# Cross-covariance attention into a channel mix: q and k kept apart in their tile, v loaded ahead, and the rows of batch 1 taken earlier

## The chip, the cores and the metric

The kernel runs on one core of a Trainium2 chip. The metric is device time of one execution in microseconds (us). Before the change three runs took 515.36, 516.77 and 517.39 us; the median is 516.77 us.

## The reference

Two layers follow one another. B is 4, N 6208, C 256; the hidden width of the second layer is 1024.

```python
qn = q / (norm(q, axis=1) + 1e-6)           # over the 6208 rows
kn = k / (norm(k, axis=1) + 1e-6)
s  = kn.transpose(0, 2, 1) @ qn / tau       # 256 x 256 for each batch
a  = softmax(s)                             # over the last axis
x  = v @ a                                  # B x N x C
xk = mu_k * x + (1 - mu_k) * x_prev         # x_prev: x one row earlier, 0 at row 0
xr = mu_r * x + (1 - mu_r) * x_prev
out = sigmoid(xr @ w_r) * (relu(xk @ w_k) ** 2 @ w_v)
```

For each batch all rows of q and k must have been read before its 256 x 256 matrix `a` exists, and `a` is needed for the first row of x.

## The kernel before, in words

The 6208 rows of a batch are 12 blocks of 512 rows and 64 rows that are left. q and k are read in *groups*: group 0 holds the 64 left rows, the others 512 rows (the last two groups of batch 0 hold 256 each). In a group, partition p holds four consecutive rows, so a group is four *units* (rows in the words of the change) of 128 rows of q and k; a unit is two matmuls into `s_ps` (L167) and, for every second unit, one squaring by ScalarE (`unit_square`, L150), which is added to the running sum of squares `acc` by VectorE (`next_add`, L154).

Batch 0 comes first and alone: its q and k are read as fp32 by SyncE's queue and cast by VectorE (`group_cast`, L131). For batches 1 to 3 GpSimd's queue reads q and k and casts to bf16 on the way (L125). It also loads v (`v_load`, L311), again with a cast. A loaded block of v is transposed: blocks 0 to 2 by TensorE (`v_transpose_pe`), later ones by a DMA transpose from SyncE's queue (`v_transpose`, L318).

The main loop has one *pass* for each i from -2 on, with eight *steps* j from 0 to 7; step (i, j) is named so below. In pass i the kernel computes `up` for block i+1 (x_k times w_k, eight pieces, L419, with a relu by ScalarE, L423, and a squaring by VectorE, L429), `down` for block i (x_r times w_r, L444, and the squared hidden layer times w_v, L448), the output of block i (tanh on ScalarE, L457; product on VectorE, L458), and x and the mixes for block i+2 (`x_half`, L348; `mix`, L404). Between these it takes units of the next batch: the tuple `slots` says in which steps, and `unit()` calls `loads_upto()`, which loads q/k groups up to three ahead of the unit. Every engine works its instructions in the order in which they are written here; the program waits only through semaphores.

The first five units of batch 1 (`early`) have their matmuls in pass -1 and their squares in passes 0 and 1 (L641). When the last unit of a batch is done, sixteen pieces (`softmax_pieces`: `evac` copies `s_ps` out, L254; `fold`, `norms`, `roots`, `roots2`, `invert`, `spread`, `scale`, `exp`, `weigh`) are done one a step. They end in `a_sb`, which `x_half` needs for the first block of the next batch, two passes after the pieces start.

Buffers that matter: five `qk` tiles, five `v_bf`, four `vT`, one `s_ps` for batches 1 to 3 (so the next batch's first matmul has to follow `evac`). GpSimd's DMAs use eight semaphores in turn, so that each of its DMAs is issued after the one eight places earlier has landed. In its queue before the loop stand: v of block 0, w_k, group 0 of batch 1 (q, then k), v of block 1, group 1, w_r, w_v, v of block 2, group 2 (L564 to L571).

Of the kernel before, what the change touches and what calls it, by code (L numbers as in the profile page):

```python
# [10 lines left out]
F32 = mybir.dt.float32  # L11
BF16 = mybir.dt.bfloat16
AX = mybir.AxisListType.X
AF = mybir.ActivationFunctionType
OP = mybir.AluOpType
# [3 lines left out]
def kernel(  # L19
# [13 lines left out]
    nc = tc.nc  # L33
    B, N, C = q.shape
    D = C
    DF = moe_w_k.shape[1]
    P = 128
    M = 512
    S = M // P
    assert C == 256 and DF == 1024  # L40
    NB = N // M
    L = N - NB * M
# [44 lines left out]
    sums = {}  # L87
# [15 lines left out]
    def qk_src(t, b, g):  # L103
        if g == 0:
            return t[b, NB * M:, :].rearrange("(p j) c -> p j c", j=1)
        r = P * sum(sizes(b)[1:g])
        n = sizes(b)[g]
        return t[b, r:r + P * n, :].rearrange("(p j) c -> p j c", p=P)

    def group_load(b, g):  # L110
        rows, n = rows_of(b, g)
        qk = pq.tile([P, S, 2, C], BF16, name="qk", tag="qk", bufs=5)
        groups[b, g] = (qk,)
        if b == 0:
            qk2 = pq.tile([P, S, 2, C], BF16, name="qk2", tag="qk2", bufs=4)
            groups[b, g] += (qk2,)
            t_f = []
            for i, t in enumerate((q, k)):
                f = pq.tile([P, S, C], F32, name=f"f{i}", tag=f"f{i}", bufs=6)
                nc.sync.dma_start(f[:rows, :n], qk_src(t, b, g))  # L120
                t_f.append(f)
            groups[b, g] += tuple(t_f)
        else:
            for i, t in enumerate((q, k)):
                nc.gpsimd.dma_start(qk[:rows, :n, i, :], qk_src(t, b, g))  # L125

    def group_cast(b, g):
        rows, n = rows_of(b, g)
        qk, qk2, *t_f = groups[b, g]
        for i in range(2):  # L130
            nc.vector.tensor_copy(qk[:rows, :n, i, :], t_f[i][:rows, :n])  # L131
        for i in range(2):
            nc.scalar.activation(qk2[:rows, :n, i, :], t_f[i][:rows, :n], AF.Square)  # L133

    def unit_square(b, g, s):

        rows, n = rows_of(b, g)
        if s % 2:
            return
        qk = groups[b, g][0]  # L140
        if n == 1:
            t = pq.tile([P, 1, 2 * C], BF16, name="sq", tag="sq1", bufs=2)
            sums[b, "left"] = t
        elif (g, s) == (1, 0):
            t = pn.tile([P, 2, 2 * C], F32, name="acc", tag="acc", bufs=2)
            sums[b] = t
        else:
            t = pq.tile([P, 2, 2 * C], F32, name="sq2", tag=f"f{s // 2}", bufs=6)
            adds.append((now[0] + 2, b, t))
        nc.scalar.activation(t[:rows], qk[:rows, s:s + min(n, 2)].rearrange("p s i c -> p s (i c)"), AF.Square)  # L150

    def next_add():
        _, b, t = adds.pop(0)
# [2 lines left out]
    def unit_matmul(b, g, s):  # L156
        rows, n = rows_of(b, g)
        t0 = g == order(b)[0] and s == 0
        te = g == len(sizes(b)) - 1 and s == n - 1
        if t0:  # L160

            cov[b] = (ps.tile([P, 2, C], F32, name="s_ps", tag="s_ps" if b else "vr_ps", bufs=1 if b else 2),
                      ps.tile([P, 2 * C], F32, name="ssq_ps", tag="vr_ps", bufs=2) if b == 0 else None)
        s_ps = cov[b][0] if b or g <= DIRECT else cov["s"]
        qk = groups[b, g][0]
        for ih in range(2):
            nc.tensor.matmul(s_ps[:, ih, :], qk[:rows, s, 1, ih * P:(ih + 1) * P],  # L167
                             qk[:rows, s, 0, :], start=t0 and ih == 0, stop=te,
                             skip_group_check=True)
        if s == n - 1 and b == 0:  # L170
            if g > DIRECT:
                norms_direct(g)
            else:
                group_norms(b, g)
# [23 lines left out]
    def softmax_pieces(b):  # L198
# [18 lines left out]
                                 start=i == 0, stop=False, skip_group_check=True)  # L217

        def fold():
            t = pq.tile([P, 2 * C], BF16, name="sq", tag="sq", bufs=1)  # L220
            nc.vector.tensor_tensor(t, sums[b][:, 0], sums[b][:, 1], op=OP.add)
            sums[b] = t

        def norms():
            bank[b] = ps.tile([P, 2 * C], F32, name="bank", tag="xT_ps", bufs=2)
            for t, rows in ((sums.pop((b, "left"))[:, 0], L), (sums.pop(b), P)):
                for i in range(4):
                    nc.tensor.matmul(bank[b][:, C + i:C + i + 1], t[:rows, i * P:(i + 1) * P], ones[:rows, 0:1],
                                     start=rows == L and i == 0, stop=rows == P, skip_group_check=True)
# [78 lines left out]
    def v_load(i):  # L308
        b, t = blocks[i]
        v_bf = p2.tile([P, S, C], BF16, name="v_bf", tag="v_bf", bufs=5)  # L310
        nc.gpsimd.dma_start(v_bf, v[b, t * M:(t + 1) * M, :].rearrange("(s p) c -> p s c", p=P))  # L311
        st[i, "v"] = v_bf
# [247 lines left out]
    def next_load():  # L560
        group_load(*loads.pop(0))
        pos["ld"] += 1

    nc.gpsimd.dma_start(w_k_sb, moe_w_k.rearrange("(ko ki) f -> ki ko f", ki=P))  # L564
    next_load()
    v_load(1)
    next_load()
    nc.gpsimd.dma_start(w_r_sb, moe_w_r.rearrange("(ko ki) d -> ki ko d", ki=P))
    nc.gpsimd.dma_start(w_v_sb, moe_w_v.rearrange("(fo fi) d -> fi fo d", fi=P))
    v_load(2)  # L570
    next_load()  # L571
    roots()
    evac()
    nc.scalar.activation(gate, ones[:, 0:1], AF.Exp)
# [13 lines left out]
    early = units[:S + 1]  # L588
# [4 lines left out]
    left = {}  # L593
    for i in range(-2, NBLK - 1):
        for j in range(8):
            if j % 2:
                if j == 1 and i >= 1:
                    finish(i - 1, 3)
                elif j > 1 and i >= 0:
                    finish(i, j // 2 - 1)  # L600
            if j == 0 and 3 <= i + 5 < NBLK - 1:
                v_load(i + 5)
            if chain:
                piece = chain[0]
                if len(chain) == FOLD and any(e[1] == holds[0] for e in adds):
                    piece = None
                else:
                    chain.pop(0)
                if piece is not None:
                    piece()  # L610
            if 0 <= i + 1 < NBLK:
                up(i + 1, j)
            if i >= 0:
                if j == 0 :
                    square(i, 7)
            if j > 0 and 0 <= i + 1 < NBLK:
                square(i + 1, j - 1)
            if j > 0 and i >= 0:
                down(i, j - 1)
            elif j == 0 and i >= 1:  # L620
                down(i - 1, 7)
            if i + 2 < NBLK:
                n = i + 2
                full = 0 < n < NBLK - 1
                if j in (0, 2) and full:
                    x_half(n, int(j > 0))
                if j == 3:
                    mix_delta(n)
                if j in (4, 5):
                    mix(n, "xk", int(j > 4))  # L630

            if j in (0, 2) and 0 <= i + 1 < NBLK:
                mix(i + 1, "xr", int(j > 0))
            if i == -1 and j == 6:
                v_transpose_pe(2, nc.vector.tensor_copy)()
            if j == 5 and 3 <= i + 4 < NBLK - 1:
                v_transpose(i + 4)
            if i == -1 and j in (5, 6):
                for u in early[:2] if j == 5 else early[2:]:
                    unit_matmul(*u)  # L640
            if (i, j) in ((0, 1), (0, 5), (1, 3)):  # L641
                unit_square(*early[{(0, 1): 0, (0, 5): 1, (1, 3): 3}[i, j]])
            if i < 0:
                slots = ()
            elif i == 0:
                slots = (3, 5, 7)
            elif i == 1:
                slots = (1, 2, 4, 5, 7)
            elif i < 8:
                slots = (1, 2, 3, 4, 5, 7)  # L650
            else:
                slots = (3, 5, 7) if (i - 8) % NB == 0 else (1, 3, 4, 5, 7) if (i - 8) % NB < 3 else (1, 3, 5, 7)
            if j in slots and pos["mm"] < len(units):
                unit()
            if adds and adds[0][0] <= now[0] and (j in (1, 6, 7) or adds[0][1] == holds[0] and chain):
                next_add()
            now[0] += 1
            if i >= 0 and i % NB == 2 and j == 1 and i // NB < B:
                left_go[0] = left_x(i // NB)
            if i >= 0 and i % NB == 4 and j == 4 and i // NB < B:  # L660
                left_go[0][0]()
            if i >= 0 and i % NB == 6 and j == 4 and i // NB < B:
                left_go[0][1]()
# [36 lines left out]
```

## Time and profile before

| what | value |
|---|---|
| median of three runs | 516.77 us (515.36 to 517.39) |
| the profiled execution | 517.02 us, of which its span is 515.2 |
| PE busy | 490.6 us, 95% |
| DVE (VectorE) busy | 457.2 us, 89% |
| ACT (ScalarE) busy | 431.3 us, 84% |
| POOL (GpSimd) busy | 104.6 us, 20% |
| POOL's DMA queue (q0) | 65808 packets, 33.01 MB |
| SyncE's DMA queue (q1) | 77712 packets, 49.98 MB |

PE is TensorE, PEld its weight loads. Busy time of PE overstates how near it is to its peak, because matmuls are pipelined. Bytes of a casting load are counted as they are written, in bf16; twice as many are read.

### The profile page before, as it was taken

The page shows a single profiled execution, that of the slowest core. Times are in us where ns is not written, and L with a number is a line of the kernel's source. Part 1 is how long each engine was busy: PE and PEld are TensorE (multiplying, and loading weights), DVE is VectorE, ACT ScalarE, POOL GpSimd, SP SyncE. Part 2 cuts the span into 40 slices and gives each one's busy share as a digit, 9 for nine tenths or more (in the row PEclk, how much of TensorE's full clock was granted, in tenths as well). Part 3 has the DMA queues.
Part 4 walks back from the last instruction along what each step waited for, and adds up shares of the span by engine and source line. Part 5 has one row for each costly group of instructions (what it writes and reads, how often), then busy time and mean ns, then how long its engine had stood idle before and what let it go on. Part 6 is the DMA issues. An engine that isn't in the chain of part 4 may idle for free.

```text
span 515.2 us, 9442 instructions
## 1 busy us (share of the span) xinstructions
PE 490.6 (95%) x3447; PEld 333.2 (65%) x3509; DVE 457.2 (89%) x788; ACT 431.3 (84%) x858; POOL 104.6 (20%) x143
## 2 busy tenths in 40 slices
PE   3988899999999999999999999999999999999996
PEld 1453666666666667667666667677666666666665
DVE  3557899999999999999999999999989788888884
ACT  5887889988988889888988898898878887878884
POOL 0045242213242321311243231210030101000000
PEclk9989999999999999999999999999999999999999
DMA  8999999999989999879899999965269676424123
GB/s 298 420 316 181 192 160 192 208 196 193 154 122 188 208 163 190 144 125 193 130 150 188 189 164 169 182 115 130 62 108 178 109 142 117 112 70 116 42 83 102
DMA packets 143734, 83.72 MB, mean 162 GB/s; under 512 B 51716, under 2 KB 140104, under 8 KB 143688
## 3 DMA queue, kind: packets, MB, share of 16 engines
q0 software_dynamic: 65808, 33.01, 51.9%
q1 hardware_dynamic: 77712, 49.98, 41.8%
q8 instruction: 27, 0.44, 0.3%
q14 instruction: 19, 0.16, 0.1%
q10 hardware_dynamic: 168, 0.13, 0.1%
HBM read 78.71 MB, written 25.43 MB: 202 GB/s over the span
## 4 chain that ended last, share of the span: by engine, by line
PE 69%; DVE 16%; DMA 9%; ACT 3%; issue 1%; POOL 0%; SPq 0%; DVEq 0%; ACTq 0%; POOLq 0%
PE vr_ps L448 26%; PE kT_ps L419 23%; PE vr_ps L444 8%; PE xT_ps L348 6%; DMA f<-in_k_dram 5%; PE s_ps L167 5%; DVE acc L154 5%; DVE kk L429 4%; DVE xk L404 2%; DMA v_bf<-in_v_dram 2%; DVE res L458 2%; DMA vT<-v_bf 2%; DVE xr L404 1%; DVE delta L394 1%; ACT kr L423 1%
## 5 line engine op out<-in xcount | busy, mean ns | idle before, releaser
L423 ACT ACTIVATE kr<-kT_ps 128x512 bf16<-128x512 f32 (+1 forms) x392 | 233.9, 600 | 41.0 <-PE kT_ps L419 36.9
L448 PE MATMUL vr_ps<-w_v_sb,kk 128*128 128x256 bf16 x1536 | 231.7, 273 | 0.9 <-DVE kk L429 0.3
L419 PE MATMUL kT_ps<-xk,w_k_sb 128*128 128x512 bf16 (+1 forms) x725 | 218.4, 377 | 0.3 <-DVE xk L404 0.2
L448 PEld LDWEIGHTS <-kk 128*128 128x128 bf16 x1536 | 149.5, 98 | 60.1 <-DVE kk L429 3.0
L429 DVE TENSOR_TENSOR kk<-kr 128x1024 bf16<-128x1024 bf16 (+1 forms) x196 | 133.0, 679 | 4.2 <-ACT kr L423 3.3
L458 DVE SCALAR_TENSOR_TENSOR res<-res,vr_ps 128x256 f32<-128x256 f32 x192 | 79.7, 415 | 28.2 <-ACT res L457 27.8
L419 PEld LDWEIGHTS <-w_k_sb 128*128 128x128 bf16 x784 | 76.1, 98 | 28.6 <-issue 0.5
L154 DVE TENSOR_TENSOR acc<-acc,sq 128x1024 f32<-128x1024 f32 x69 | 84.0, 1217 | 0.0
L167 PE MATMUL s_ps<-qk 128*128 128x256 bf16 (+1 forms) x392 | 74.0, 291 | 5.4 <-DVE qk L131 5.4
L457 ACT ACTIVATE res<-vr_ps 128x256 f32<-128x256 f32 x192 | 75.4, 393 | 1.3 <-PE vr_ps L448 1.3
L444 PE MATMUL vr_ps<-w_r_sb,xr 128*128 128x256 bf16 x384 | 73.2, 272 | 3.1 <-DVE res L458 0.4
L350 ACT CAST xT<-xT_ps 128x512 bf16<-128x512 f32 x94 | 55.8, 594 | 23.3 <-PE xT_ps L348 23.1
L150 ACT ACTIVATE sq<-qk 128x1024 f32<-128x1024 bf16 (+1 forms) x72 | 75.2, 1046 | 0.0
L404 DVE SCALAR_TENSOR_TENSOR xr<-delta,mu_t,xT 128x512 bf16<-128x512 bf16 x96 | 71.4, 744 | 0.0
L404 DVE SCALAR_TENSOR_TENSOR xk<-delta,mu_t,xT 128x512 bf16<-128x512 bf16 x96 | 71.3, 745 | 0.0
L444 PEld LDWEIGHTS <-xr 128*128 128x128 bf16 x384 | 37.5, 98 | 45.4 <-issue 1.4
L125 POOL DMA_DIRECT2D qk<-in_q_dram x39 | 28.7, 736 | 181.1 <-ACT kr L423 140.5
L348 PE MATMUL xT_ps<-vT,a_sb 128*128 128x512 bf16 x188 | 56.1, 379 | 4.1 <-DVE a_sb L273 2.2
L311 POOL DMA_DIRECT2D v_bf<-in_v_dram x48 | 37.2, 777 | 67.8 <-DMA vT<-v_bf 62.6
L167 PEld LDWEIGHTS <-qk 128*128 128x128 bf16 (+1 forms) x392 | 39.0, 103 | 17.9 <-DVE qk L131 8.2
L394 DVE TENSOR_TENSOR delta<-xT 128x1024 bf16<-128x1024 bf16 x48 | 32.9, 686 | 0.1
L133 ACT ACTIVATE qk<-f 128x1024 bf16<-128x1024 f32 (+2 forms) x28 | 25.9, 947 | 7.4 <-DMA f<-in_q_dram 4.1
(82 smaller groups left out, 164.1 us busy)
## 6 DMA issues: line engine op xcount, KB each, us to landing
out_dram<-res SPq DMA_DIRECT2D x47, 512.0 KB, 5.2
v_bf<-in_v_dram POOLq DMA_DIRECT2D x48, 256.0 KB, 7.7
qk<-in_q_dram POOLq DMA_DIRECT2D x36, 256.0 KB, 6.3
qk<-in_k_dram POOLq DMA_DIRECT2D x36, 256.0 KB, 7.4
f<-in_q_dram SPq DMA_DIRECT2D x11, 512.0 KB, 8.4
f<-in_k_dram SPq DMA_DIRECT2D x11, 512.0 KB, 9.3
vT<-v_bf SPq DMA_TRANSPOSE x45, 7.9
f<-in_q_dram SPq DMA_DIRECT2D x2, 256.0 KB, 8.3
```

The lines of the kernel that those rows point to most:

```text
L150: nc.scalar.activation(t[:rows], qk[:rows, s:s + min(n, 2)].rearrange("p s i c -> p s (i c)"), AF.Square)
L154: nc.vector.tensor_tensor(sums[b], sums[b], t, op=OP.add)
L167: nc.tensor.matmul(s_ps[:, ih, :], qk[:rows, s, 1, ih * P:(ih + 1) * P], qk[:rows, s, 0, :], start=t0 and ih == 0, stop=te, skip_group_che ...
L348: nc.tensor.matmul(xT_ps, a_sb[:, b, ih, dh * P:(dh + 1) * P], vT[:, :, ih, :], start=ih == 0, stop=ih == 1)
L404: nc.vector.scalar_tensor_tensor(o[:, dh], st[i, "d"][:, dh], mu[:, dh:dh + 1], st[i, "x"][:, dh, :M], op0=OP.mult, op1=OP.add)
L419: nc.tensor.matmul(kT_ps[:, :m], w_k_sb[:, dh, fh * P:(fh + 1) * P], xk[:, dh, :m], start=dh == 0, stop=dh == 1)
L423: nc.scalar.activation(st[i, "kr", fh // 2][:, fh % 2, :m], kT_ps[:, :m], AF.Relu, scale=0.5 ** 0.5)
L429: nc.vector.tensor_tensor(st[i, "kk"][:, fh - 1:fh + 1, :m], kr, kr, op=OP.mult)
L444: nc.tensor.matmul(vr_ps[:, D:], xr[:, dh, s * P:(s + 1) * P], w_r_sb[:, dh, :], start=dh == 0, stop=dh == 1)
L448: nc.tensor.matmul(vr_ps[:, :D], kk[:, fh, s * P:(s + 1) * P], w_v_sb[:, fh, :], start=fh == 0, stop=fh == 7)
L457: nc.scalar.activation(res[:, s], vr_ps[:, D:], AF.Tanh, scale=0.5)
L458: nc.vector.scalar_tensor_tensor(res[:, s], res[:, s], 1.0, vr_ps[:, :D], op0=OP.add, op1=OP.mult)
```

## The change

1. In the tile of a q/k group, q and k stand apart: `[P, 2, S, C]` in place of `[P, S, 2, C]`. A partition's four rows of q are then one run of 2048 bytes in the tile, where there were four of 512, and the same for k. Squares, sums, fold, norms and matmuls are indexed accordingly.
2. GpSimd's queue: v of block 1 stands ahead of group 0, v of block 2 ahead of w_r and w_v, v of block 3 ahead of group 2, and v of block 4 ahead of group 3. Group 2 moves from before the loop to pass -2, group 3 from pass 0 to pass -1.
3. The squares of the early units are taken in steps (0,0), (0,2) and (0,4), not (0,1), (0,5) and (1,3). Pass 0 takes four units, one of them in step 1, where it took three; pass 1 takes six where it took five. All later units come up to two slots earlier, so that the last unit of batch 1 falls in step (7,4) in place of (7,7), that of batch 2 in (19,3) in place of (19,7), that of batch 3 in (31,3) in place of (31,7), and the softmax pieces start accordingly.

```diff
     def group_load(b, g):
-        qk = pq.tile([P, S, 2, C], BF16, name="qk", tag="qk", bufs=5)
+        qk = pq.tile([P, 2, S, C], BF16, name="qk", tag="qk", bufs=5)
...
-                nc.gpsimd.dma_start(qk[:rows, :n, i, :], qk_src(t, b, g))
+                nc.gpsimd.dma_start(qk[:rows, i, :n, :], qk_src(t, b, g))
     def group_cast(b, g):
...
-            nc.vector.tensor_copy(qk[:rows, :n, i, :], t_f[i][:rows, :n])
+            nc.vector.tensor_copy(qk[:rows, i, :n, :], t_f[i][:rows, :n])
     def unit_square(b, g, s):
...
-            t = pq.tile([P, 2, 2 * C], F32, name="sq2", tag=f"f{s // 2}", bufs=6)
+            t = pq.tile([P, 2, 2, C], F32, name="sq2", tag=f"f{s // 2}", bufs=6)
...
-        nc.scalar.activation(t[:rows], qk[:rows, s:s + min(n, 2)].rearrange("p s i c -> p s (i c)"), AF.Square)
+        nc.scalar.activation(t[:rows], qk[:rows, :, s:s + min(n, 2)], AF.Square)
...
         def fold():
-            nc.vector.tensor_tensor(t, sums[b][:, 0], sums[b][:, 1], op=OP.add)
+            nc.vector.tensor_tensor(t, sums[b][:, :, 0], sums[b][:, :, 1], op=OP.add)
...
     nc.gpsimd.dma_start(w_k_sb, moe_w_k.rearrange("(ko ki) f -> ki ko f", ki=P))
-    next_load()
     v_load(1)
     next_load()
+    next_load()
+    v_load(2)
     nc.gpsimd.dma_start(w_r_sb, moe_w_r.rearrange("(ko ki) d -> ki ko d", ki=P))
     nc.gpsimd.dma_start(w_v_sb, moe_w_v.rearrange("(fo fi) d -> fi fo d", fi=P))
-    v_load(2)
-    next_load()
...
             if j == 0 and 3 <= i + 5 < NBLK - 1:
                 v_load(i + 5)
+                if i < 0:
+                    next_load()
...
-            if (i, j) in ((0, 1), (0, 5), (1, 3)):
-                unit_square(*early[{(0, 1): 0, (0, 5): 1, (1, 3): 3}[i, j]])
+            if (i, j) in ((0, 0), (0, 2), (0, 4)):
+                unit_square(*early[{(0, 0): 0, (0, 2): 1, (0, 4): 3}[i, j]])
             if i < 0:
                 slots = ()
             elif i == 0:
-                slots = (3, 5, 7)
-            elif i == 1:
-                slots = (1, 2, 4, 5, 7)
+                slots = (1, 3, 5, 7)
             elif i < 8:
                 slots = (1, 2, 3, 4, 5, 7)
```

More of the change, by code (lines that the diff above doesn't have):

```diff
@@ L141, in unit_square @@
         if n == 1:
-            t = pq.tile([P, 1, 2 * C], BF16, name="sq", tag="sq1", bufs=2)
+            t = pq.tile([P, 2, 1, C], BF16, name="sq", tag="sq1", bufs=2)
             sums[b, "left"] = t
         elif (g, s) == (1, 0):
-            t = pn.tile([P, 2, 2 * C], F32, name="acc", tag="acc", bufs=2)
+            t = pn.tile([P, 2, 2, C], F32, name="acc", tag="acc", bufs=2)
             sums[b] = t
         else:
-            t = pq.tile([P, 2, 2 * C], F32, name="sq2", tag=f"f{s // 2}", bufs=6)
+            t = pq.tile([P, 2, 2, C], F32, name="sq2", tag=f"f{s // 2}", bufs=6)
             adds.append((now[0] + 2, b, t))
-        nc.scalar.activation(t[:rows], qk[:rows, s:s + min(n, 2)].rearrange("p s i c -> p s (i c)"), AF.Square)
+        nc.scalar.activation(t[:rows], qk[:rows, :, s:s + min(n, 2)], AF.Square)
     def next_add():
@@ L166, in unit_matmul @@
         for ih in range(2):
-            nc.tensor.matmul(s_ps[:, ih, :], qk[:rows, s, 1, ih * P:(ih + 1) * P],
-                             qk[:rows, s, 0, :], start=t0 and ih == 0, stop=te,
+            nc.tensor.matmul(s_ps[:, ih, :], qk[:rows, 1, s, ih * P:(ih + 1) * P],
+                             qk[:rows, 0, s, :], start=t0 and ih == 0, stop=te,
                              skip_group_check=True)
@@ L219, in fold @@
         def fold():
-            t = pq.tile([P, 2 * C], BF16, name="sq", tag="sq", bufs=1)
-            nc.vector.tensor_tensor(t, sums[b][:, 0], sums[b][:, 1], op=OP.add)
+            t = pq.tile([P, 2, C], BF16, name="sq", tag="sq", bufs=1)
+            nc.vector.tensor_tensor(t, sums[b][:, :, 0], sums[b][:, :, 1], op=OP.add)
             sums[b] = t
@@ L225, in norms @@
             bank[b] = ps.tile([P, 2 * C], F32, name="bank", tag="xT_ps", bufs=2)
-            for t, rows in ((sums.pop((b, "left"))[:, 0], L), (sums.pop(b), P)):
+            for t, rows in ((sums.pop((b, "left")).rearrange("p i s c -> p (i s c)"), L),
+                            (sums.pop(b).rearrange("p i c -> p (i c)"), P)):
                 for i in range(4):
```

## The prediction

> **What bounds the kernel now.** I read the page first: shares, then the chain that ended last.
>
> ```profile
> PE 490.6 (95%) x3447; PEld 333.2 (65%) x3509; DVE 457.2 (89%) x788; ACT 431.3 (84%) x858; POOL 104.6 (20%) x143
> PE 69%; DVE 16%; DMA 9%; ACT 3%; issue 1%; POOL 0%; SPq 0%; DVEq 0%; ACTq 0%; POOLq 0%
> ```
>
> PE carries most, but DVE (16%) and DMA (9%) carry stages of their own. The busy times by stretch show which:
>
> ```profile
> 50.00:60.00 10.00, 8.74 (x64) 5.78 (x64) 8.32 (x14) 7.56 (x15) 4.46 (x6) 1.00 1.45 196
> 60.00:70.00 10.00, 8.02 (x56) 5.37 (x56) 8.45 (x13) 8.53 (x18) 2.24 (x3) 1.00 1.42 173
> 100.00:120.00 20.00, 19.62 (x139) 13.37 (x140) 20.00 (x33) 17.84 (x36) 5.59 (x8) 1.00 1.40 186
> 200.00:220.00 20.00, 19.89 (x141) 13.81 (x142) 19.58 (x34) 17.79 (x36) 4.07 (x6) 1.00 0.98 158
> 460.00:480.00 20.00, 19.84 (x140) 13.55 (x142) 16.25 (x29) 16.26 (x36) 0.00 (x0) 1.00 0.31 80
> ```
>
> (Columns: stretch, length, busy us of PE, weight loads, DVE, ACT, POOL, clock, DMA share, GB/s.) At 50 to 70 us every engine has holes. While six rows of batch 1 are mixed into each block (100 to 120) DVE is full: 20.00 of 20. Later PE is full. The starts of each block's first relu give one loop pass: 10.39 us with six rows, 9.56 with four, 8.68 with none. So a row costs PE 0.22 us, (9.56-8.68)/4. In the chain an add (L154) holds DVE 1.14 us, so the DVE pass without its three adds is 10.39-3.42 = 6.97.
>
> The chain in order of time and PE's waits show the hole and the other stalls:
>
> ```profile
> 44.80 11.06 DMA v_bf<-in_v_dram
> 55.88 9.37 DMA vT<-v_bf
> 65.29 0.59 PE xT_ps L348 x2
> ```
>
> ```profile
> PE xT_ps L348 <- DVE a_sb L273: 2.2, 3, 0.9
> PE xT_ps L348 <- DMA vT<-v_bf: 1.9, 1, 1.9
> PE vT_ps L327 <- DMA v_bf<-in_v_dram: 1.2, 1, 1.2
> ```
>
> v of block 3 took 11 us to land and 9 more to be transposed; PE waited 1.9 for it and 1.2 for v of block 2. The softmax of the next batch (a_sb) came late three times (0.92, 0.91, 0.38).
>
> Last, the DMA view of two stretches: 37 to 39 us, where only w_k is moved (2 KB packets, as the changed q and k get), and 43 to 59, where 512 B packets are.
>
> ```profile
> DMA packets 156, 0.32 MB, mean 160 GB/s; under 512 B 0, under 2 KB 0, under 8 KB 156
> DMA packets 6263, 3.14 MB, mean 196 GB/s; under 512 B 185, under 2 KB 6260, under 8 KB 6260
> ```
>
> The wide packets were slower. A 256 KB load costs the queue 1.34 us at 196 GB/s and 1.64 at 160.
>
> **What the Trainium skill says.** "Perfetto Trace Analysis", section DMA Optimizations, calls transfers under 2 KB costly and promises gains from larger ones; the rows above say the opposite for casting loads. "DMA: Bandwidth & Descriptors", section Queues, rings and completion order: a DMA engine goes round its queues packet by packet. The trace agrees: from 60 to 65 us, with a transpose beside the loads, 1244 packets went on the POOL queue and 1211 on the other. "VectorE: DVE Perf Modes", the perf-mode tier table: a copy with an fp32 operand in SBUF has at most the 2x mode, so I expect no gain for the casts from a contiguous output (694 ns now; bound 0.5 to 0.9, hidden behind batch 0's loads, for which DVE waits 12.4 us).
>
> **The change part by part.** I write x for the queue time of a 256 KB q or k load: 1.34 before; I take 1.45 (w_k's median packet of 173 ns, 8 to each of 16 engines, is 1.39; its mean rate 1.64); ends 1.1 (a gain from fewer packets) and 2.2.
>
> *Layout.* Square, adds and matmuls keep their numbers of elements and contiguous rows: nothing (an add is contiguous still; fold's two-strip read costs at most 0.1 in three places). POOL issues 0.74 us as before, w_k's being 0.81.
>
> *Order of loads.* POOL may have eight DMAs outstanding (each later one waits for the eighth before). Before: w_k, group 0, v1, group 1, w_r, w_v, v2, group 2, v3, v4. After: w_k, v1, group 0, group 1, v2, w_r, w_v, v3, group 2, v4, group 3. The queue is served in order and is full from 41 to 60 us, so landings (from the trace's semaphore records) shift by what was moved. v2 (51.84 before) lands near 48.7; its wait goes. But DVE, busy without a gap from 50.80 to 53.40 (mixes, a kk, the copy of vT), still releases L348 for block 2 at about 53.45 instead of 53.86: 0.4 gained, not 1.2. w_v now waits until w_k has landed (42.3), but its queue place, behind v2, gives 50.51+1.34+0.2 = 52.1, before its first use near 54.5: hidden by 2.4 us of up matmuls and v2's transposes, and past that PE would wait us for us.
>
> Group 2 is the new wait. Its k landed at 54.58; now v3 is ahead (+1.34) and four wide loads cost 4(x-1.34) = 0.45 more: 56.4 (55.9 at x=1.34, 57.1 at 1.64). Its first unit moves from step (0,3) to (0,1), where PE arrives at 55.1 (first L448 at 54.95, 0.4 earlier, three matmuls). PE waits 1.3 us, and ACT with it, since the square of group 2 stands in ACT's queue before the next relus. Then ACT has to do, until block 2's first relu, five squares at 0.95, six relus at 0.55, a cast 0.55, three tanh at 0.35: 9.65, so 66.05. The next relu, after a copy and a cast, follows at 67.3; before it was at 66.68, held by vT. So +0.6 (from -0.6 without the wait, to +1.3 at 57.1).
>
> vT of block 3: v3 lands at 53.4 instead of 55.86. Its packets begin 4 us after the issue, as before: 57.4. It needs 1024 turns against v4, group 3, v5, group 4: 612 turns with narrow packets at 249 a us, 2.5, and 412 with wide ones at 0.0129 us, 5.3: lands at 65.2, when PE asks near 66. The 1.9 wait goes, with little to spare; the ACT line above already takes its place.
>
> *More rows early.* Four rows in pass 0, six in pass 1. The adds up to the end of pass 1 are five in both, so DVE, which bounds from 70 us on, gets no more until pass 7. Batch 1's rows end two slots earlier, at (7,4). DVE in passes 7 to 10: 6.97 + three adds + fold 0.6 = 11.0; + two adds, roots, invert 1.1 = 10.35; + two adds, scale and weigh 1.3 = 10.55; 10.39; sum 42.3 against 41.94 measured (11.00+9.62+11.17+10.15): +0.4. One add more falls in these passes. Also batch 2's first matmul now follows evac (0.58, L254) in the same step, where four steps lay between: ACT owes square 0.95, tanh 0.35, evac 0.55 while PE has 1.0 of work: PE waits up to 0.9, half hidden as DVE bounds: +0.4. Together +0.8 (0 to 1.5). Queued behind that matmul are the next up and down matmuls.
>
> *Batches 2 and 3.* The chain of pieces starts four steps earlier, so a_sb is in time: of 0.91 I take 0.6 (DVE is near-full in passes 20 to 22, two adds now in 20), and 0.4 in batch 3. Two rows fewer in pass 31: 0.44.
>
> Sum: +0.6 +0.8 -0.6 -0.4 -0.44 = 0.0. The profiled execution is 517.02 (span 515.2, 1.8 around it), 0.25 above the median 516.77; I predict 516.7.
>
> **Rivals.**
> (a) DMA becomes the bound of batch 1: slower. A block of 10.39 us must move three q/k loads, one v (1.34), stores and a transpose (0.31 of 8.68 us in the 460 to 480 row, 2.7). 3x+4.0 reaches 10.39 at x=2.1; there group 2 is already 2.6 later, 519.3; at 2.2, 0.3 more a block over seven blocks and 0.4 at the start: 521.8. For: wide packets slow at 160 GB/s, DMA share 1.40 now. Against: it needs packets of 260 ns, w_k's mean was some 190.
> (b) Wide packets are quicker, x at 1.1: group 2 lands at 55.0, no wait, -0.6; DVE's holes at 66.83 and 70.38 (0.35, 0.73) close, -1.1; +0.4 in batch 1; -1.44 later: 514.0. For: a quarter of the packets. Against: the view above.
> (c) The packets stay 512 B: x=1.34, group 2 at 55.9: 516.2.
> (d) The shifts fail: DVE holds passes 20 to 22 (-0.6 gone), evac is not hidden (+0.7), group 2 at 57.1 (+0.7), vT later than 66 (+0.5): 519.2.
>
> **How the numbers follow.** Forecast 0.46, (a) 0.12, (b) 0.14, (c) 0.10, (d) 0.18. 0.5% is 2.6 us, about what a measurement here can tell: below 514.2 faster, above 519.4 slower. (b) ends at that line and gives faster 0.14; (a), half of (d) and the forecast's upper tail 0.28 slower; the rest 0.58. The range runs from (b)'s middle, 514.0, to between (d) and (a), 520.2; the forecast alone is 515.4 to 518.2.
>
> **What would show it.** Right: q/k packets of 2 KB at about 1.45 us a load; PE or ACT waiting near 55 us for the DMA of q/k group 2; no vT wait at 65; the a_sb waits gone; PE waiting for evac once, near 137. Wrong: q/k loads of over 2 us each or vT waits in several blocks (a); no wait at 55 and DVE full from 62 (b); a_sb still awaited at 276 (d).

## The result, and the profile after

| | runs | median us | range |
|---|---|---|---|
| before | 4 | 516.08 | 515.36 to 517.39 |
| after | 4 | 519.11 | 518.50 to 519.35 |

The ratio is 1.0054 (95% interval 1.0028 to 1.0080): the changed kernel is 0.3 to 0.8% slower, where 516.7, no change, was forecast. The profiled execution of after took 519.35 us, its span 517.6. (Ratios here leave out executions more than 1.5% above the fastest of their kernel; medians don't.)

From the page of after: busy times, GpSimd's DMA queue, and the chain that ended last.

```profile
PE 491.8 (95%) x3447; PEld 332.7 (64%) x3509; DVE 457.3 (88%) x788; ACT 432.0 (83%) x858; POOL 89.4 (17%) x143
...
q0 software_dynamic: 38160, 33.01, 43.5%
...
PE 41%; DVE 3%; issue 1%; ACT 1%; DVEq 0%
```

The totals of the three compute engines are those of before within 1.2 us, so the loss is no added work: it is when the work falls. The queue carries the same bytes in 38160 packets instead of 65808. The chain is followed back only to 280 us, so it says nothing of the start. Busy times in the stretches that were shown of before (same columns):

```profile
50.00:60.00 10.00, 8.14 (x58) 5.29 (x58) 6.24 (x11) 8.40 (x16) 2.65 (x5) 1.00 1.21 200
60.00:70.00 10.00, 9.76 (x70) 6.79 (x71) 10.00 (x16) 10.00 (x20) 3.41 (x6) 1.00 1.27 177
100.00:120.00 20.00, 19.68 (x136) 13.21 (x137) 20.00 (x32) 17.84 (x36) 4.06 (x7) 1.00 0.92 159
```

From 60 us on the holes are gone, but from 50 to 60 VectorE (third value) works 6.24 us where it worked 8.32, and after that it is full, with no room to catch up. The waits for `DMA vT<-v_bf`, `DMA v_bf` and `DVE a_sb` that were shown of before are gone. VectorE's longest wait for a tanh of ScalarE (`DVE res <- ACT res`) has grown from 1.0 to 2.7 us.

The DMA view of 49 to 51 us, where half of the packets are wide and carry most of the bytes (from 43 to 59 us the mean is 199 GB/s):

```profile
DMA packets 335, 0.42 MB, mean 211 GB/s; under 512 B 29, under 2 KB 166, under 8 KB 334
```

From the starts of each block's first relu, which bound one pass each, the time by stages (worked out from the traces; the two runs on the right are experiments below):

| passes | before, profiled | before, second trace | after | rows alone | loads alone |
|---|---|---|---|---|---|
| before -1 | 46.62 | 46.43 | 46.32 | 46.45 | 45.40 |
| -1 to 2 | 38.21 | 36.96 | 38.01 | 38.01 | 36.54 |
| 3 to 6 | 41.65 | 41.65 | 41.65 | 41.65 | 41.65 |
| 7 to 11 (end of batch 1) | 51.68 | 51.68 | **54.02** | **53.86** | 51.67 |
| 12 to 18 | 67.02 | 67.02 | 67.02 | 67.02 | 67.02 |
| 19 to 23 (batch 2) | 50.15 | 50.15 | **50.76** | **50.99** | 50.15 |
| 24 to 30 | 67.02 | 67.02 | 67.02 | 67.02 | 67.02 |
| 31 to 34 (batch 3) | 37.06 | 37.06 | 36.93 | 36.93 | 37.06 |
| 35 to 46 | 103.25 | 103.25 | 103.25 | 103.25 | 103.25 |

Stages away from the edited places repeat to 0.01 us in these traces. The end of batch 1 costs 2.34 us, that of batch 2 0.61, that of batch 3 gains 0.13. The stretch before the first relu is 45.4 to 47.7 over all traces, whatever the kernel; and passes -1 to 2 of the profiled execution of before, with its waits for v and vT, were 1.25 us longer than those of its second trace.

The window of passes 7 to 11, before, then after:

```profile
126.48:178.16 51.68, 49.91 (x351) 33.98 (x357) 51.10 (x88) 45.12 (x91) 14.75 (x18) 1.00 1.13 169
```

```profile
125.97:180.00 54.03, 50.60 (x351) 33.96 (x357) 52.12 (x89) 45.45 (x92) 14.08 (x21) 1.00 0.94 165
```

VectorE does 1.02 us more (52.12 against 51.10: one add more, x89 for x88), and is idle for 1.91 instead of 0.58. That is the whole of it: 1.02 + 1.33 = 2.35. The waits of after from 125 to 172 us (us in total, times, longest):

```profile
DVE res L459 <- ACT res L458: 1.8, 1, 1.8
...
PE bank L229 <- DVE sq L221: 0.8, 1, 0.8
...
PE bank L252 <- DVE rq_d L247: 0.6, 1, 0.6
PE s_ps L167 <- ACT s_sb L255: 0.6, 1, 0.6
```

Three of the batch's softmax pieces now hold TensorE, which works in order: norms (L229) waits for fold, which stands in VectorE's queue behind four adds in pass 7; spread (L252) waits for invert; the first row of batch 2 waits for evac. In the same stretch of before no piece but the last (a_sb, 0.9) held it.

VectorE's idle time itself is the first line of that list: one wait of 1.81 us, in pass 9, for block 9's first tanh. ScalarE works without a gap ahead of that tanh, and the two exps of batch 1's softmax (L267) stand in its queue there:

```profile
151.57 1.07 ACT L150 ACTIVATE sq<-qk 128x1024 f32<-128x1024 bf16 x1
152.51 0.52 ACT L267 ACTIVATE s_sb<-s_sb,rn 128x256 f32<-128x256 f32 x1
...
153.00 0.51 ACT L267 ACTIVATE s_sb<-s_sb,rn 128x256 f32<-128x256 f32 x1
...
153.50 0.60 ACT L424 ACTIVATE kr<-kT_ps 128x512 bf16<-128x512 f32 x1
153.97 0.60 ACT L351 CAST xT<-xT_ps 128x512 bf16<-128x512 f32 x1
154.44 0.42 ACT L458 ACTIVATE res<-vr_ps 128x256 f32<-128x256 f32 x1
```

```profile
154.89 0.42 DVE L459 SCALAR_TENSOR_TENSOR res<-res,vr_ps 128x256 f32<-128x256 f32 x1 [1.81 <-ACT res L458]
```

In before the exps come only after block 9's second tanh (at 154.38), and VectorE waits 0.32 us for the first:

```profile
154.38 0.38 ACT L457 ACTIVATE res<-vr_ps 128x256 f32<-128x256 f32 x1
154.64 0.51 ACT L266 ACTIVATE s_sb<-s_sb,rn 128x256 f32<-128x256 f32 x1
```

### The profile page after: what moved, and what is told of

Same layout as the page of the kernel before. It is cut to its first block, busy times and chain, and to the rows that moved or that the text cites. A ratio compares the mean times of both kernels' runs of the same rounds, so it can differ in the third digit from the quotient of the medians.

```text
span 517.6 us, 9444 instructions
## 1 busy us (share of the span) xinstructions
PE 491.8 (95%) x3447; PEld 332.7 (64%) x3509; DVE 457.3 (88%) x788; ACT 432.0 (83%) x858; POOL 89.4 (17%) x143
## 3 DMA queue, kind: packets, MB, share of 16 engines
q0 software_dynamic: 38160, 33.01, 43.5%
## 5 line engine op out<-in xcount | busy, mean ns | idle before, releaser
L125 POOL DMA_DIRECT2D qk<-in_q_dram x39 | 21.0, 539 | 199.2 <-ACT kr L424 139.4
```

## The experiments

There are two theories. Theory one: taking the rows early makes batch 1 end where VectorE is full, so its pieces and an add fall badly, and that is the whole loss; layout and loads are harmless. Theory two: wide packets or the order of the loads cost later.

### First group: one part at a time

*The change with the rows as before* (pass 7 ends the batch at (7,7) again; layout and loads changed):

```diff
-            if (i, j) in ((0, 0), (0, 2), (0, 4)):
+            if (i, j) in ((0, 1), (0, 5), (1, 3)):
...
-                slots = (1, 3, 5, 7)
+                slots = (3, 5, 7)
+            elif i == 1:
+                slots = (1, 2, 4, 5, 7)
```

> The changed kernel with its third part undone: squares of the early units and slots of passes 0 and 1 as before; layout and order of loads changed. Theory 1 (the two slots' earlier end of each batch is what costs, because its pieces then fall where VectorE is behind; layout and loads gain 0.5 us at the start): 0.5 to 1.5 us faster than the kernel before, passes 7 to 10 again about 41.9 us. Theory 2 (the layout or the loads cost later, in every block): at least 1.5 us slower than the kernel before.

Measured: 528.93 (523.79 to 538.13), ratio 1.0171 (1.0136 to 1.0206). Theory one's forecast of a kernel faster than before failed.

*Before with the rows alone*: the lines above the other way round, in the kernel before.

> The kernel before with the third part of the change alone. Theory 1: 2.3 us more in passes 7 to 11, 0.6 in passes 19 to 23, nothing gained at the start: 2.5 to 3.5 us slower than before. Theory 2: within 0.7 us of before.

Measured: 519.27, ratio 1.0067 (1.0047 to 1.0088). The rows alone give the changed kernel's time and, within 0.25 us, its stages (table above), with the same waits.

*The change with the end of batch 1 moved back*: pass 7 takes four rows, spread so that the last is again in (7,7).

```diff
+            elif i == 7:
+                slots = (1, 3, 5, 7)
             elif i < 8:
```

> The changed kernel with four units in pass 7 in place of six, so that each batch ends in the step where it ended before; the early start stays. Theory 1: the start's 0.5 us stays gained, pass 7 gives back about 0.8 more (four units, not six, where VectorE bounds), passes 8 to 11 as before: 0.5 to 1.8 us faster than before. Theory 2: at least 1.5 us slower than before, since layout and loads are untouched.

Measured: 515.86 in one run, 527 to 532 in three; none is faster than before, as theory one had it. In its trace, of the execution of 531.66, passes 7 to 11 take 51.55, so this edit does undo the loss there; but passes 12 to 18 take 82.58 instead of 67.02.

*Before with the layout alone*: `[P, 2, S, C]` and its indices in the kernel before.

> The kernel before with q and k apart in the tile, loads and rows as before. Theory 1: 0 to 1 us faster than before, from wide packets that land the early loads sooner (a 256 KB load near 1.28 us of queue time). Theory 2, if it is the layout: at least 1.5 us slower.

Measured: 525.8, ratio 1.0183 (1.0152 to 1.0213).

The three kernels with 2 KB packets all lost time in the same way, whatever their schedule. From the wait list of the one with the end moved back:

```profile
PE xT_ps L349 <- DMA vT<-v_bf: 11.5, 5, 3.2
```

The transposes of v landed too late in some passes (16.8 us over nine waits with rows as before, 8.7 over four with the layout alone). The changed kernel's own trace has no such wait. So theory one holds for the loss seen in the result, since the rows alone give it, and theory two names something that the changed kernel might show as well.

### Second group

*The changed kernel again.*

> The changed kernel unaltered, beside the three other kernels of this group. In its own runs it took 519.1 us, with passes 7 to 11 of the steady stages 2.3 us longer than before and every later pass between the ends of batches the length it had. The two wide-tile kernels that leave the rows of batch 1 elsewhere (the rows as before; batch 1's end moved back) took 524 to 538 us with VectorE's v copies waiting for transposes. If the wide tile alone delays transposes in some runs, this kernel shows it here too: above 522 us, with waits for vT of more than 1 us in its trace. If the delay needs the other order of rows, this kernel takes 519 us again (518.3 to 519.6), without a vT wait above 0.5 us.

Measured: 523.3 (520.58 to 530.99), ratio 1.0145 (1.0107 to 1.0183). The traced execution, the one of 530.99, does show it; the other three, also longer than any of the first runs, have no trace:

```profile
PE xT_ps L349 <- DMA vT<-v_bf: 12.2, 5, 4.0
```

*Tile narrow, loads and early rows as changed, end of batch 1 moved back* (the edit of pass 7 above, with `[P, S, 2, C]`).

> The tile layout of before, the loads in the changed order, the first rows of batch 1 early as in the change, but only four row tiles in pass 7, so that batch 1's softmax begins where it did before. If the earlier end of batch 1 is the cost (theory one), passes 7 to 11 take 51.7 us as before, the early rows keep a gain of 0.3 to 0.8 at the start, and the kernel takes 0.3 to 1.2 us less than before: ratio 0.9975 to 0.9995. If the early rows themselves or the load order cost (theory two), it is 1 us or more above before.

Measured: 516.5, ratio 1.0028 (1.0010 to 1.0046): slower, against theory one's forecast. Yet passes 7 to 11 take 51.68, batches 2 and 3 50.15 and 37.06, all as before. Left is the start: passes -1 to 2 take 38.00.

*Loads alone.*

```diff
-    next_load()
     v_load(1)
     next_load()
+    next_load()
+    v_load(2)
```

(and so on as in the change, with layout and rows of before)

> Before with the order of the loads alone changed (v of blocks 1 to 3 ahead of the groups); tile layout and rows as before. Both theories of the loss: theory one (the end of batch 1) expects 0.5 us less to 0.5 us more than before, since v of block 2 and 3 comes earlier while groups 1 and 2 come later, and rows are needed only from pass 0, step 1 on. Theory two (loads) expects 1 us or more above before, with the loss in passes 0 to 3.

Measured: 514.72, ratio 1.0001 (0.9985 to 1.0017): no difference, as theory one expected. Its passes -1 to 2 take 36.54.

*Rows alone, and the pieces of batch 1 held four steps.*

```diff
+        if b == 1:
+            return [evac, None, None, None, None, fold, None, norms, roots, roots2, None, invert, None, spread, scale,
+                    None if bounded else top, exp, None, weigh]
```

> Before with the rows of batch 1 alone taken early (which took 519.3, ratio 1.0067), and in batch 1 four more steps between the copy of the logits and the sum of the norms, so that VectorE has finished the three adds of pass 7 before the norms, the inversion and the spread are issued. If TensorE loses time because these pieces fall where VectorE is behind, the waits at the norms (0.82 us) and at the spread (0.49) become under 0.3 us and the kernel takes about 1.3 us less than with the rows alone: 517.5 to 518.5 on the scale where before is 515.8; the 0.6 us wait for the copy of the logits stays. If the time is lost to the larger number of rows in passes 7 and 8 as such, and the waits only show where the engines meet, the time stays at 519 to 519.6 and the waits move elsewhere.

Measured: 518.34, ratio 1.0067 (1.0052 to 1.0083). The ratio is that of the rows alone, so the kernel's time doesn't show a gain. Traces differ in the start by more than the 1 us at stake, so the stage is what tells: 52.81 us, 1.05 less than with rows alone.

```profile
126.79:179.60 52.81, 50.27 (x351) 33.95 (x357) 52.23 (x89) 45.42 (x92) 16.98 (x21) 1.00 1.09 162
```

VectorE's idle time is back at 0.58; the 1.13 that stay are its busy time. TensorE's wait for norms is gone, that for spread still 0.4, that for evac still 0.6 and harmless: VectorE is full beside it. The exps stand behind block 9's first two tanh again, and VectorE waits 0.32 us for the first, as before.

### Third group

*The kernel before again*, one run.

> The kernel before once more, for a second trace of its start. The profiled execution that the prediction was worked from took 517.02, above most others (515.2 to 515.5), and in it the first weights' load took 8.2 us from issue to landing where every later trace shows 6.0. If that execution's start was an exception, this one has no wait for v of block 2 (1.2 us there) and none or less for the transpose of block 3 (1.9 there), the passes from 0 to 2 take 1 to 2 us less, and what the changed loads seemed to gain at the start was no gain over a usual start. If the waits belong to the kernel, both are here again.

Measured: 515.59, passes -1 to 2 in 36.96, 1.25 less than in the execution that the prediction used. The waits at the start are there, but about half as long:

```profile
PE xT_ps L348 <- DMA vT<-v_bf: 1.1, 1, 1.1
...
PE vT_ps L327 <- DMA v_bf<-in_v_dram: 0.5, 1, 0.5
```

So the waits belong to the kernel and their size doesn't: each answer of the expectation was half right. The first weights' load landed at 41.66 us here, at 42.30 in the prediction's trace, at 41.78 in the changed kernel's second trace, and at 39.3 to 41.0 in most others.

*The changed kernel with 512 B packets in the wide tile*: row tile j holds other rows of the group.

```diff
-        return t[b, r:r + P * n, :].rearrange("(p j) c -> p j c", p=P)
+        return t[b, r:r + P * n, :].rearrange("(j p) c -> p j c", p=P)
```

> The changed kernel, with q and k of batches 1 to 3 read so that row tile j holds rows j*128 to j*128+127 of the group (sums over rows do not depend on which partition holds which row): the tile stays wide, and the packets become 512 B again, as before. If the 2 KB packets make the transposes late (waits for vT of 1 to 4 us in the four wide kernels of the last two groups, none in the narrow ones), this one has no vT wait above 0.5 us and takes 518.3 to 519.6, as the rows alone did. If the tile's layout or something else in the order of work does it, it is above 521 with vT waits.

Measured: 520.19, ratio 1.0097 (1.0078 to 1.0115), no wait for vT, but 0.6 above the range. Here the first weights landed late (42.27), and TensorE waited for k of group 2:

```profile
PE s_ps L174 <- DMA qk<-in_k_dram: 1.1, 1, 1.1
```

*Rows alone, pass 7 with four rows packed in steps 1 to 4*, so that the batch ends as early but no row of batch 2 follows until pass 8; and *pieces held, with one of batch 2's adds left out*. One run each.

```diff
+            elif i == 7:
+                slots = (1, 2, 3, 4)
```

```diff
         _, b, t = adds.pop(0)
+        if b == 2 and not left_out:
+            left_out.append(b)
+            return
```

> Before with the rows of batch 1 alone taken early, but pass 7 takes four row tiles, in steps 1 to 4, so that batch 1 ends as early as in the change and no row of batch 2 follows until pass 8. Passes 7 to 11 took 51.68 us before and 53.86 with the rows early (three quarters of a pass more in pieces; VectorE 51.10 busy before, 51.95 and 1.9 idle after; one add of 1.22 us more). If the added add and the early pieces each cost about 1.1, this leaves the pieces only: 52.5 to 53.2. If the wait for the copy of the logits (0.62) costs by itself, 52.2 to 52.6. If what matters is only how many adds fall in, 51.4 to 51.9.

> The kernel with the rows early and the pieces of batch 1 held by four steps (passes 7 to 11: 52.81 us, VectorE idle for 0.58 of them as before), with one of VectorE's adds of batch 2 left out, so that the norms of batch 2 lack two row tiles. If the rest of the loss is one add of 1.22 us more on a full VectorE, passes 7 to 11 take 51.5 to 51.9, as before the change (51.68). If it is TensorE's wait of 0.62 for the copy of the logits, they stay at 52.6 to 52.9.

Passes 7 to 11, the packed one, then the held one:

```profile
126.19:179.95 53.76, 50.63 (x354) 33.46 (x353) 51.12 (x88) 44.36 (x90) 14.09 (x18) 1.00 1.04 163
```

```profile
126.00:178.17 52.17, 50.44 (x358) 33.96 (x357) 50.98 (x88) 45.31 (x91) 16.98 (x21) 1.00 1.13 167
```

Both lie outside their ranges. With early pieces, an add and two units less (VectorE 51.12 busy) are worth only 0.10, because VectorE then idles for 2.64: the pieces' place decides by itself. In this packed kernel TensorE waits neither for spread nor for evac, yet VectorE waits the same 1.81 us for block 9's first tanh, which again stands behind the exps:

```profile
154.63 0.42 DVE L458 SCALAR_TENSOR_TENSOR res<-res,vr_ps 128x256 f32<-128x256 f32 x1 [1.81 <-ACT res L457]
```

So the waits for spread and evac don't make that idle time. The place of the exps and TensorE's wait for norms (1.0 us here) are left; holding the pieces moves both, and no run here separates them. With the pieces held, an add less is worth 0.64, and 0.49 above before stays.

### Fourth group

*The changed kernel a third time, and beside it the same kernel with 512 B packets.*

> The changed kernel once more, beside its twin with 512 B packets on the same chip. It took 519.1 in its own runs without a vT wait, and 520.6 to 531 on another chip with vT waits of up to 4 us. If the 2 KB packets cause the late transposes but only in some executions, the spread is again wide here, or one of the two times is above 521; if the first runs were typical, 518.5 to 519.5. In every case passes 7 to 11 cost 2.2 to 2.4 us more than before, apart from vT waits.

> The changed kernel with row tile j read as rows j*128 and on, so that the packets of q and k are 512 B; the tile stays wide. It took 519.4 to 520.6 on its first chip, without vT waits. If the packets are what makes the transposes late, this one stays at 518.5 to 520.6 without vT waits above 0.5 us, whatever the kernel beside it does; if it is the chip or the tile, both go up together.

Measured: 518.71, ratio 1.0074 (1.0053 to 1.0096), and 519.02, ratio 1.0074 (1.0054 to 1.0094). Neither has a vT wait; both take 53.86 for passes 7 to 11. So the result stands on a third set of runs. The pair didn't meet transposes so late that TensorE waits. But it does show what the packets do to a transpose: that of block 3, issued between 50 and 52 us, took from issue to landing, in us, with 2 KB packets and then with 512 B:

```profile
vT<-v_bf SPq DMA_TRANSPOSE x1, 12.1
```

```profile
vT<-v_bf SPq DMA_TRANSPOSE x1, 9.0
```

The other traces agree without exception: 12.1 to 14.9 us in the six with 2 KB packets, 8.9 to 9.4 in the thirteen with 512 B; and the longest transpose whose landing is recorded took 16.5 to 22.3 us in the six, 11.2 to 12.9 in the thirteen.

*Pieces held and pass 7 with four packed rows*, one run.

> Rows early, pass 7 with four row tiles in steps 1 to 4, and the pieces of batch 1 held by four steps. Passes 7 to 11 took 51.68 before, 53.86 with rows early, 53.76 with four packed rows, 52.81 with the pieces held, 52.17 with the pieces held and an add left out. If the early pieces (at most 1.7) and the added add (0.1 to 0.6) are what costs, and the wait for the copy of the logits (0.62) is covered by VectorE, this takes 52.0 to 52.3, like the kernel with an add left out. If that wait is the half microsecond left, 51.5 to 51.8.

```profile
126.08:178.24 52.16, 49.77 (x354) 33.70 (x353) 50.97 (x88) 44.13 (x90) 14.73 (x18) 1.00 1.11 165
```

52.16, as forecast: the wait for evac is gone and the half microsecond is not. Holding the pieces is worth 1.60 here (53.76 to 52.16). VectorE is busy for 50.97, no more than before, and idle for 1.19, against 0.58.

*The narrow kernel with the end moved back, one square of ScalarE replaced by a fill on GpSimd.*

```diff
+        if (b, g, s) == (1, 1, 2):
+            nc.gpsimd.memset(t[:rows], 0.0)
+            return
         nc.scalar.activation(t[:rows], ...
```

> The kernel with narrow tile, changed loads, early rows and batch 1's end moved back (516.5; passes -1 to 2 took 38.01 us, against 36.54 with the loads alone and 36.96 in the second trace of before), where the square of one early pair of row tiles is replaced by a fill with zeros on GpSimd, so that the norms of batch 1 lack two row tiles; VectorE's add of it stays. If the start is bound by ScalarE once four rows are squared in pass 0 (five squares of 0.97 us there, and no idle time in pass 1), passes -1 to 2 take 36.9 to 37.4. If VectorE's adds or TensorE's rows cost it, 37.7 to 38.1.

Measured: passes -1 to 2 in 38.01, so this square's time isn't it. But VectorE still waited 2.7 us for block 0's first tanh, and the square that went stood behind that tanh. The timeline of ScalarE in the changed kernel (start, us, line; two or more alike in one row):

```profile
55.28 1.99 ACT L150 ACTIVATE sq<-qk 128x1024 f32<-128x1024 bf16 x2
57.17 0.58 ACT L424 ACTIVATE kr<-kT_ps 128x512 bf16<-128x512 f32 x1
57.65 0.57 ACT L351 CAST xT<-xT_ps 128x512 bf16<-128x512 f32 x1
58.11 1.06 ACT L150 ACTIVATE acc<-qk 128x1024 f32<-128x1024 bf16 x1
59.07 0.37 ACT L458 ACTIVATE res<-vr_ps 128x256 f32<-128x256 f32 x1
```

and with the loads alone:

```profile
55.25 0.59 ACT L350 CAST xT<-xT_ps 128x512 bf16<-128x512 f32 x1 [0.31 <-PE xT_ps L348]
55.73 0.39 ACT L457 ACTIVATE res<-vr_ps 128x256 f32<-128x256 f32 x1
56.01 0.60 ACT L423 ACTIVATE kr<-kT_ps 128x512 bf16<-128x512 f32 x1
56.49 2.01 ACT L150 ACTIVATE sq<-qk 128x1024 f32<-128x1024 bf16 x2
```

Step (0,1) puts group 2's two squares, and step (0,2) the first square of the sums, ahead of the tanh (`res`), which starts 6.6 us after the pass's first relu, against 4.2 with the loads alone. VectorE, in order, stands behind it:

```profile
59.48 0.42 DVE L459 SCALAR_TENSOR_TENSOR res<-res,vr_ps 128x256 f32<-128x256 f32 x1 [2.71 <-ACT res L458]
```

*The same narrow kernel, again four rows in pass 0, the squares after the tanh.*

```diff
-            if (i, j) in ((0, 0), (0, 2), (0, 4)):
+            if (i, j) in ((0, 1), (0, 5), (0, 7)):
...
             elif i == 0:
-                slots = (1, 3, 5, 7)
+                slots = (3, 4, 5, 7)
```

> The kernel with narrow tile, changed loads, early rows and batch 1's end moved back, with the same four row tiles in pass 0, but taken in steps 3, 4, 5 and 7, and the early squares at steps 1, 5 and 7, so that the squares of ScalarE no longer stand ahead of the first tanh of block 0. With them ahead, VectorE waited 2.71 us for that tanh and passes -1 to 2 took 38.00 us (36.54 with the loads alone, 36.96 in the second trace of before). If those squares, by their place, cost the start, the wait shrinks to about 0.8 and passes -1 to 2 take 36.4 to 37.0, the kernel 515 or less. If the number of rows in pass 0 costs it, 37.7 to 38.1 and 516.5.

Measured: passes -1 to 2 in 36.99, no wait for a tanh above 0.85, the first tanh again 4.2 us after the first relu; 515.38, a little above the forecast 515, ratio 1.0012 (0.9999 to 1.0026). The place of the squares, moved here together with their rows, cost 1.0 of the 1.46 us. The number of rows is left with at most 0.45. Nothing here points to a kernel better than before: loads alone and this one are its equals.

## Why the prediction was wrong

- **Failed step, "DVE in passes 7 to 10 ... +0.4".** The prediction saw that one add more falls there, and priced an add at 1.14. But it set a modelled sum for after (42.3) against a measured one for before (41.94). The same model of before (9 adds, three pieces' sums) gives 4 x 6.97 + 9 x 1.14 + 3.0 = 41.1, 0.8 too little, and that shortfall swallowed most of the add. Model against model, the term is +1.14, as an add is; measured, VectorE's busy time over passes 7 to 11 grew by 1.02.
- **Failed step, pieces without a term.** "Together +0.8" priced evac's wait (0.4) and no other. Evac's wait came, 0.6 us long at 134 us, and cost nothing where VectorE was full. What cost is idle time of VectorE, +1.33, nearly all in one wait for a tanh that stands behind the exps, pieces to which the prediction gave no term. Holding the pieces by half a pass takes all of it back (1.92 to 0.58 with the rows alone). TensorE's wait for norms may have a part in it, which isn't shown. In place of +0.8, +2.34.
- **Failed step, "Batches 2 and 3", -0.6 and -0.4, and -0.44 for pass 31.** The a_sb waits went, as foreseen, but the passes didn't shorten: +0.61 and -0.13. Why is open; in batch 2 VectorE's busy time is the same (47.90 in passes 19 to 23 before, 47.89 after), so the loss there is idle time.
- **Start, +0.6: the sign is right against a usual start (+1.05), the reason wrong.** Against its own execution it is -0.20, since these passes took 1.25 us more in that execution than in the second trace. All landings were shifted from it: group 2 was put at 56.4 and landed at 52.80, of which 2.75 is the weights' landing (42.30 against 39.55) and about 0.8 x. The wait for group 2 exists, and came once when the weights were late (1.1 us, with 512 B packets). The real cost, squares ahead of the first tanh, is in the prediction's own count of ScalarE's queue; it took them for a sum, where their order mattered.
- **x.** Landings of group 2 and 3 are 1.23 to 1.44 us apart, those not beside a transpose 1.23 to 1.25. Taken was 1.45, near w_k's 8 packets of 173 ns one after another, 1.39. The packets do take 172 ns, but they overlap: from 50 to 52 us of the third run their times sum to 111.7% of the engines' time, and 1.39 / 1.117 is 1.24. Rival (b), at 1.1, had the direction, and its signs came (no wait for group 2, VectorE full from 60 us), but not its gain. Of the Trainium skill's "Perfetto Trace Analysis", section DMA Optimizations, the direction is confirmed, and the size is small: 1.34 to 1.24 us for 256 KB, no dramatic gain.
- **vT of block 3.** Forecast 65.2, landed 62.66, no wait. The reasoning was right: v had landed early, and from issue to landing 11.8 us were forecast, 12.3 measured, against 9.4 before.
- **Rival (d)** (shifts fail, 519.2) came nearest by luck: of its four parts only the lost gain of batch 2 came. Evac cost nothing, group 2 landed at 52.80 and not 57.1, vT at 62.66 and not after 66, and a_sb wasn't awaited. Rival (a)'s sign, "vT waits in several blocks", came in one of the changed kernel's three sets of runs (523.3), with its loads of group 2 1.2 to 1.3 us apart and not 2.1.

Summed: against the second trace of before, +1.05 (start), +2.34, +0.61, -0.13 = +3.87; the medians differ by 3.03 in the first runs and 3.58 in the last.

**What stays open.** The 0.5 us of passes 7 to 11 that remains with pieces held and an add less: it is idle time of VectorE, most of it at one tanh (a wait of 0.7 us, before 0.3). The loss of batch 2. And the late transposes: six traces of kernels with 2 KB packets, four with vT waits in several passes, two without; thirteen with 512 B packets, none beyond block 3. That wide packets slow the transposes is shown, by the pair and by all traces; that they alone make TensorE wait isn't, since the pair met no such wait, nor why some runs are spared.

## What to carry to other kernels

When an engine is full, an instruction moved into its stretch counts almost in full (1.02 us for an add of 1.14); price it as an increment, model against model, never a modelled sum against a measured one. Work that is moved earlier in an in-order queue moves everything behind it: ask which result stands behind it (here a tanh behind three squares, and another behind two exps) and which engine has no slack to take the delay. And look at the start of a second execution before crediting a change with a wait that it removes.

## What the runs showed of the hardware

- Casting loads of 256 KB in 2 KB packets took about 1.24 us of queue time, in 512 B packets 1.30 to 1.34: a packet of 2 KB took 172 ns (median, 60 to 130 us), one of 512 B 60, both with overlap (111.7% and 144.0% of the engines' time from 50 to 52 us in the pair), and the queue's share of the engines fell from 51.9 to 43.5%.
- GpSimd issues a q load of four runs per partition in 736 ns on average, of one run in 539: its busy time fell from 104.6 to 89.4 us.
- A DMA transpose beside these loads (that of block 3) took 12.1 to 14.9 us from issue to landing with 2 KB packets and 8.9 to 9.4 with 512 B, in all nineteen traces.
- In one trace with late transposes (the changed kernel's second, 60 to 130 us), nine in ten of the transposes' 256 B packets took up to 115 ns, against 31 in its first trace, and the slowest 2 KB packet 6.6 us against 2.3.
